# A decode step with its gradients: engine orders by hand, job loads on ScalarE, and w4 summed in the last forward heads

## The chip, the cores and the metric

The kernel runs on one core of a Trainium2 chip. The metric is the device time of one execution in microseconds (us), from the first to the last instruction with what lies around them. The time before the change is the median of three runs.

## The reference

One token (a vector of D = 640) goes through a block that a vector c conditions, and the function returns the block's output and the gradients of it against nine inputs. Cut to what matters:

```
mod = silu(c) @ w_mod                       # six vectors sa, ca, ga, sb, cb, gb of 640
h = layernorm(x) * (1 + ca) + sa
q = h @ wq                                  # 32 heads of 192
p = softmax(q . k_cache * 192**-0.5)        # 8192 keys a head
x1 = x + ga * ((p . v_cache) @ wo)
hb = layernorm(x1) * (1 + cb) + sb
out = x1 + gb * (hb + gelu(layernorm(hb) @ w3) @ w4)
```

The second block of the reference also has weights w1 and w2, but its shifted groups are all zero for a sequence of one token, so they add nothing. The gradients, for a given gradient of out, are those of x, k_cache, v_cache, wq, wo, w3, w4, c and w_mod. The two caches are 100 MB each in bf16; both are read (V twice, K once), and gradients of their size are written.

## The kernel before, in words

The keys of a head are laid over 128 partitions, 64 keys each, in two halves t = 0, 1 of 32 keys; a half of K or V is one DMA of 1.5 MB. The program has three stages.

**Forward (L395 to L444).** An iteration i works on three heads at once. Head i gets its scores: K times q on VectorE in four quarters (`prod`, L308 through L93), summed over 192 by ScalarE (`junk`, L313) for two quarters and by TensorE (`S_ps`, L316) for the other two. Head i-1 gets the maximum of its scores over all keys (L320 to L329, `mx_ps` and `negm`), its exp (`E_all`, L330), then `W` = V times E on VectorE (W0 and W1 for the halves, L93), and two products on TensorE that contract the keys of K with W: M1 (L349) for the first 128 of K's 192 columns and M2 (L363) for the rest. M1 and M2 hold what the gradient of q needs; by M2 also the attention's output comes out, through columns of K that GpSimd overwrites with ones (L354) after M1 has read them. Head i-2 gets its last M2 and its evictions and output (`fwd_out`). K halves use five buffers (`KV_sb`), V halves two. All these loads are issued by SyncE, in one queue: K (L159), V (L297), and in odd iterations W_o (L169), 480 KB of wo for this pair of heads, and W_c (L164), 480 KB of wq for the next pair's q. `q_bcast` makes q of two heads at a time (L264 on TensorE, L265 on ScalarE). In heads 1 to 6 a chunk of w_mod, also a `W_c`, is loaded and multiplied (`mod_chunk`, L248, with its copy L249).

**Middle (L450 to L568).** w4 and w3 are loaded, x1, two layernorms, w3, gelu, its derivative and the gradients back to `dao_c`, the gradient of the attention's projected output. The gradient that reaches gelu is a sum of w4 times a vector (`dg_part`, L470, twelve of them on VectorE).

**Backward (L749 to L787).** An iteration i loads V of head i again and multiplies it by `do_t` (L720 to L729, `dP_ps`), writes dV and dK as outer products by VectorE (`head_dv` L730, `head_dk` L734, issued from GpSimd, L714). The jobs of a pair of heads come beside it, every one and a half iterations: `pair_a` (L603) transposes W_o by TensorE (L612) and makes `do_t` and `qb_t`; `pair_b1` and `pair_b2` make the softmax's correction and the gradient of q; `pair_c` makes the gradients of wq and wo, `o_c` (L582) and `o_r` (L588), by ScalarE and writes them in ScalarE's DMA queue (L583, L589). Jobs for w_mod, w4 and w3 come in the last iterations.

What sets the order of the work: a scheduler of the framework takes the instructions in program order, and puts them in its own order on each engine's queue. Semaphores between engines and buffers decide when they start. The queues that matter here are SyncE's DMA queue (q1), ScalarE's (q10), GpSimd's (q0), and the instruction streams of the five engines.

Of the kernel before, what the change touches and what calls it, by code (L numbers as in the profile page):

```python
# [20 lines left out]
def kernel(  # L21
# [65 lines left out]

    V_ = nc.vector
# [73 lines left out]
    def load_cols(view, n):  # L162
        tl = ld.tile([P, NDC, CW], BF16, name="W_c", tag="ld")
        nc.sync.dma_start(out=tl, in_=view[:, :, n * CW : (n + 1) * CW])  # L164
        return tl

    def load_wo(g):
        tl = ld.tile([P, 3, D], BF16, name="W_o", tag="ld")
        nc.sync.dma_start(out=tl, in_=wo_v[g])  # L169
        return tl  # L170


    def colsum(vec, groups, out):
        ps = psum.tile([P, 512], FP32, tag="sm", name="cs_ps")
        n = groups * NDC
        PE_.matmul(ps[:, 0:n], lhsT=mean_f, rhs=vec, start=True, stop=True)
        V_.reduce_sum(out=out, in_=ps[:, 0:n].rearrange("p (g i) -> p g i", i=NDC), axis=AX.X)

    def layernorm(x_c, pfx, hook=None):
        mean = cvec(pfx + "_mean", 1)  # L180
        colsum(x_c, 1, mean)
        if hook:
            hook()
# [5 lines left out]
        colsum(sq, 1, var)  # L189
        if hook:  # L190
            hook()
        rstd = cvec(pfx + "_rstd", 1)
        std = cvec(pfx + "_std", 1)
        A_.activation(out=std, in_=var, func=ACT.Sqrt, bias=eps_c, scale=1.0)
        V_.reciprocal(out=rstd, in_=std)
# [4 lines left out]
    def layernorm_bwd(dn2, n, rstd, add_to, pfx):  # L200
        tt(dn2[:, 1, :], dn2[:, 0, :], n, ALU.mult)
        s = cvec(pfx + "_s", 2)
        colsum(dn2.rearrange("p g i -> p (g i)"), 2, s)
# [12 lines left out]
    def store_cols(dram_5p, col_f, name):  # L216
        ps = psum.tile([P, 512], FP32, tag="sm", name="st_ps")
# [25 lines left out]
    def mod_chunk(n):  # L243
        wt = load_cols(wm_v, n)
# [5 lines left out]

    n0, r0 = layernorm(x0_c, "ln0")
    NM0 = 4
    for n in range(NM0):
        mod_chunk(n)
# [12 lines left out]
    fq_cm = tc.tile_pool(name="fq", bufs=2)  # L267
# [3 lines left out]
    def q_pair(g):  # L271
        q_tiles[g] = fq.tile([P, CW], BF16, name="q_t")
        q_bcast(load_cols(wq_v, g), "q", q_tiles[g], bufs=1)

    q_pair(0)
# [9 lines left out]
    fp_cm = tc.tile_pool(name="fp", bufs=3)  # L285
    fp = fp_cm.__enter__()
    fv_cm = tc.tile_pool(name="fv", bufs=2)
    fv = fv_cm.__enter__()
    fw_cm = tc.tile_pool(name="fw", bufs=2)
    fw = fw_cm.__enter__()  # L290
    fsm_cm = tc.tile_pool(name="fsm", bufs=2)
    fsm = fsm_cm.__enter__()
# [7 lines left out]
    def fwd_mult(h, qi, st):  # L300
# [8 lines left out]
        if r == 0:  # L309
            for jj in range(JQ):  # L310
                j = qi * JQ + jj
                junk = fsm.tile([P, DH], BF16, name="junk")
                A_.activation(out=junk, in_=prod[:, jj, :], func=ACT.Copy, accum_out=st["S_h"][:, j : j + 1])  # L313
        else:
            for k in range(NDS):
                PE_.matmul(st["S_ps"][:, t, :, :], lhsT=ident_bf, rhs=prod[:, :, k * DS : (k + 1) * DS], start=(k == 0), stop=(k == NDS - 1))  # L316
# [26 lines left out]
    def fwd_m1(h, t, st):  # L343
        if t == 0:
# [3 lines left out]
        for j in range(JH):  # L348
            PE_.matmul(st["M1"][:, 0:DP], lhsT=kv[:, j, 0:P], rhs=W[:, j, 0:DP], start=(t == 0 and j == 0), stop=(t == 1 and j == JH - 1))  # L349
        if h % 2 == 0:  # L350
            ones = bass.AP(Kt.tensor, Kt.offset + DH, [list(Kt.ap[0]), [DH, JH], [1, 64]])
        else:
            ones = kv[:, :, 64:P]
        nc.gpsimd.memset(ones, 1.0)  # L354

    def fwd_m2(h, t, st):
        if t == 0:
# [4 lines left out]
        for j in range(JH):  # L362
            PE_.matmul(st["M2"][:, 0:DP], lhsT=Kt[:, j * DH + o : j * DH + o + P], rhs=W[:, j, 0:DP], start=(t == 0 and j == 0), stop=(t == 1 and j == JH - 1))  # L363

    def fwd_out(h, st):
        lo, olo = (0, 64) if h % 2 == 0 else (64, 0)
        g = h // 2
        A_.copy(out=M1_all[:, h, :], in_=st["M1"][:, 0:DP])
        oe = fsm.tile([1, DP], FP32, name="oe")
        A_.copy(out=oe, in_=st["M2"][olo : olo + 1, 0:DP])  # L370
        A_.copy(out=M2_all[lo : lo + 64, g, :], in_=st["M2"][lo : lo + 64, 0:DP])
        V_.reciprocal(out=rinv_all[0:1, h : h + 1], in_=oe[0:1, DH:DP])  # L372
        o_h = oe
        if h % 2 == 0:
            states["ops", g] = psum.tile([P, 512], FP32, tag="sm", name="o_ps")
        ops = states["ops", g]
# [372 lines left out]
    for i in range(-2, HQ):  # L749
# [27 lines left out]
        if i >= 0:  # L777
            head_dv(i)
# [40 lines left out]
```

## Time and profile before

| | |
|---|---|
| median of three runs | 1605.99 us (1593.37 to 1610.15) |
| profiled execution, its own time | 1602.02 us |
| its span | 1600.2 us |
| mean granted TensorE clock | 0.777 |
| busy: PE, DVE, ACT, POOL | 972.5, 1202.8, 619.6, 186.3 us |
| DMA moved | 574.62 MB, mean 359 GB/s |

How to read it: the stages lie one after another in the span, with the start until about 20 us, the forward loop until about 664, the middle until about 732 and the backward loop to the end. The busy times are sums over stages that have different limits, so each stage is read by itself. A DMA share is the mean busy share of the 16 DMA engines in a stretch. Names are those of the program (`KV_sb`, `V_sb`, `W_c`, ...), and L93 is a helper that records every tensor_tensor, so its rows are told apart by their tiles.

### The profile page before, as it was taken

To read this page: it belongs to the slowest core of one execution; us is meant where nothing else is said; L and a number is where in the kernel's file an instruction comes from. 1 tells how busy PE (TensorE), PEld (TensorE's weight loads), DVE (VectorE), ACT (ScalarE), POOL (GpSimd) and SP (SyncE) were. 2 spreads that over 40 slices of the span, in tenths; PEclk is the share of its full clock that TensorE was granted. 3 is DMA by queue.
4 is the path that set the end of the run, shared out by engine and by line. 5 is a ranking of instruction groups with operands and counts; after the bars stand their busy time and mean duration, and the time that the engine had idled before them with its cause. 6 is when DMAs were issued, how large, how long until landed. Compare 5 with 4: busy or idle time off the path is not lost.

```text
span 1600.2 us, 23161 instructions
## 1 busy us (share of the span) xinstructions
PE 972.5 (61%) x9043; PEld 823.7 (51%) x9043; DVE 1202.8 (75%) x1018; ACT 619.6 (39%) x2598; POOL 186.3 (12%) x203
## 2 busy tenths in 40 slices
PE   4878888888888888858444554464535563332541
PEld 3777777777777777856323342343324342222431
DVE  4677777666776666647994999399939998595977
ACT  5656666666666666423221312021302111312320
POOL 0111111111111111200100010000000001000010
PEclk9989999999999999978666676576657666566765
DMA  9789888888888888866998999899989999899998
GB/s 365 299 308 356 337 333 339 341 340 341 340 336 328 336 334 330 318 239 211 422 425 330 416 415 423 332 404 416 424 332 401 422 422 423 309 416 408 359 387 349
DMA packets 123115, 574.62 MB, mean 359 GB/s; under 512 B 7422, under 2 KB 81406, under 8 KB 82046
## 3 DMA queue, kind: packets, MB, share of 16 engines
q1 hardware_dynamic: 76798, 347.23, 55.9%
q0 software_dynamic: 18528, 201.34, 30.0%
q10 hardware_dynamic: 27680, 24.58, 4.4%
q8 instruction: 71, 1.16, 0.3%
q14 instruction: 38, 0.31, 0.0%
HBM read 347.21 MB, written 225.91 MB: 358 GB/s over the span
## 4 chain that ended last, share of the span: by engine, by line
DMA 45%; PE 22%; DVE 13%; ACT 9%; issue 7%; POOL 2%; SPq 1%; ACTq 0%; POOLq 0%; DVEq 0%
DMA W_o<-in_A_wo_dram 16%; DMA out_dram<-o_r 10%; DMA out_dram<-o_c 10%; DMA V_sb<-in_A_v_cache_dram 8%; PE M_ps L349 8%; ACT junk L313 6%; PE M_ps L363 4%; DVE W L93 3%; PE dP_ps L727 3%; DVE dK L93 2%; DVE KV_sb L93 2%; DVE prod L93 2%; POOL KV_sb L354 2%; ACT o_c L582 1%; PE S_ps L316 1%
## 5 line engine op out<-in xcount | busy, mean ns | idle before, releaser
L313 ACT ACTIVATE junk<-prod 128x192 bf16<-128x192 bf16 x1024 | 354.9, 349 | 121.1 <-DVE prod L93 121.1
L93 DVE TENSOR_TENSOR W<-V_sb,E_all 128x6144 bf16<-128x6144 bf16 x64 | 214.4, 3350 | 105.7 <-ACT E_all L330 102.4
L727 PE MATMUL dP_ps<-KV_sb,ident_bf 128*128 128x256 bf16 x1536 | 228.8, 320 | 99.5 <-DVE KV_sb L93 99.3
L349 PE MATMUL M_ps<-W,KV_sb 128*128 128x193 bf16 x2048 | 222.5, 271 | 69.8 <-DVE rinv_all L372 68.4
L727 PEld LDWEIGHTS <-ident_bf 128*128 128x128 bf16 x1536 | 174.9, 115 | 148.1 <-issue 74.2
L93 DVE TENSOR_TENSOR prod<-KV_sb,q_t 128x3072 bf16<-128x3072 bf16 x128 | 219.2, 1743 | 40.5 <-DMA KV_sb<-in_A_k_cache_dram 29.3
L349 PEld LDWEIGHTS <-KV_sb 128*128 128x128 bf16 x2048 | 200.0, 108 | 81.3 <-issue 75.2
L363 PE MATMUL M_ps<-W,KV_sb 128*128 128x193 bf16 x2048 | 194.7, 251 | 43.9 <-POOL KV_sb L354 43.2
L93 DVE TENSOR_TENSOR dV<-E_all,do_t 128x6144 bf16<-128x6144 bf16 x64 | 213.6, 3353 | 5.8 <-DMA out_dram<-dV 5.3
L93 DVE TENSOR_TENSOR KV_sb<-KV_sb,do_t 128x6144 bf16<-128x6144 bf16 x64 | 214.4, 3350 | 0.0
L93 DVE TENSOR_TENSOR dK<-dS,qb_t 128x6144 bf16<-128x6144 bf16 x64 | 212.1, 3352 | 2.7 <-DMA out_dram<-dK 2.6
L363 PEld LDWEIGHTS <-KV_sb 128*128 128x128 bf16 x2048 | 175.0, 99 | 57.0 <-POOL KV_sb L354 54.5
L313 ACT ACTIVATION_READ_ACCUMULATOR junk<-prod 128x1 f32 x1024 | 192.5, 188 | 0.0
L354 POOL MEMSET KV_sb<- 128x2048 bf16 x64 | 115.5, 1804 | 569.6 <-PE M_ps L349 556.1
L316 PE MATMUL S_ps<-prod,ident_bf 128*128 128x128 bf16 x1536 | 104.7, 225 | 11.1 <-DVE prod L93 11.1
L612 PE MATMUL wo_ps<-ident_bf,W_o 128*128 128x128 bf16 x240 | 21.3, 247 | 139.4 <-DMA W_o<-in_A_wo_dram 134.2
L666 ACT ACTIVATE vc<-dq_ps 128x384 bf16<-128x384 f32 x16 | 8.0, 498 | 250.8 <-PE dq_ps L664 250.8
L316 PEld LDWEIGHTS <-ident_bf 128*128 128x128 bf16 x1536 | 95.2, 101 | 12.5 <-issue 12.2
L612 PEld LDWEIGHTS <-W_o 128*128 128x128 bf16 x240 | 17.7, 111 | 144.5 <-DMA W_o<-in_A_wo_dram 139.2
L714 POOL DMA_DIRECT2D out_dram<-dK x64 | 34.0, 532 | 479.2 <-DVE dK L93 433.6
L736 DVE TENSOR_REDUCE dP<-dP_ps 128x64 f32<-128x512 f32 x32 | 21.9, 684 | 73.8 <-PE dP_ps L727 73.8
L582 ACT ACTIVATE o_c<-vc,ha_c 128x384 bf16<-128x384 bf16 x80 | 42.9, 604 | 70.1 <-DMA out_dram<-o_c 69.9
(198 smaller groups left out, 873.1 us busy)
## 6 DMA issues: line engine op xcount, KB each, us to landing
KV_sb<-in_A_k_cache_dram SPq DMA_DIRECT2D x64, 1536.0 KB, 8.3
V_sb<-in_A_v_cache_dram SPq DMA_DIRECT2D x64, 1536.0 KB, 11.2
KV_sb<-in_A_v_cache_dram SPq DMA_DIRECT2D x64, 1536.0 KB, 21.2
out_dram<-dV POOLq DMA_DIRECT2D x64, 1536.0 KB, 13.4
out_dram<-dK POOLq DMA_DIRECT2D x64, 1536.0 KB, 12.5
W_c<-in_A_wq_dram SPq DMA_DIRECT2D x32, 480.0 KB, 13.0
W_o<-in_A_wo_dram SPq DMA_DIRECT2D x32, 480.0 KB, 12.0
out_dram<-o_c ACTq DMA_DIRECT2D x30, 480.0 KB, 16.9
```

The costliest lines, as they stand in the source:

```text
L93: V_.tensor_tensor(out=out, in0=a, in1=b, op=op)
L313: A_.activation(out=junk, in_=prod[:, jj, :], func=ACT.Copy, accum_out=st["S_h"][:, j : j + 1])
L316: PE_.matmul(st["S_ps"][:, t, :, :], lhsT=ident_bf, rhs=prod[:, :, k * DS : (k + 1) * DS], start=(k == 0), stop=(k == NDS - 1))
L349: PE_.matmul(st["M1"][:, 0:DP], lhsT=kv[:, j, 0:P], rhs=W[:, j, 0:DP], start=(t == 0 and j == 0), stop=(t == 1 and j == JH - 1))
L354: nc.gpsimd.memset(ones, 1.0)
L363: PE_.matmul(st["M2"][:, 0:DP], lhsT=Kt[:, j * DH + o : j * DH + o + P], rhs=W[:, j, 0:DP], start=(t == 0 and j == 0), stop=(t == 1 and j ...
L582: A_.activation(out=o[:, i, :], in_=vec_bc, func=ACT.Copy, scale=col_f[:, i : i + 1])
L612: PE_.transpose(tps[:, k * P : (k + 1) * P], wo_t[:, cc, i * P : (i + 1) * P], ident_bf)
L666: A_.activation(out=v, in_=bps[:, 0:CW], func=ACT.Copy, scale=SCALE)
L714: nc.gpsimd.dma_start(out=dst_hd[h][:, t * JH : (t + 1) * JH, :], in_=o)
L727: PE_.matmul(dP_ps[:, t * JH : (t + 1) * JH, :], lhsT=ident_bf, rhs=V_sb[:, :, k * DS : (k + 1) * DS], start=(k == 0), stop=(k == NDS - 1))
L736: V_.reduce_sum(out=dP, in_=js.pop(("dP", h)), axis=AX.X)
```

## The change

The kernel is recorded in manual mode: the order of instructions on every engine is the order of the program's text, and the text is rewritten for it. The parts:

- The forward iteration is one function, `fwd_iter`, in which the three heads' steps are set by hand. The memset that puts ones over K is split in two, each after the half of M1 that read those columns; M2 is split in the same way. `q_pair` and `mod_chunk` come after the second quarter's sum and before exp. The pools of products and q lie on the other side of memory.
- w4 is loaded in iteration 32 (`tail_loads`), and nine of the twelve `dg_part` run between iterations 32 and 33. The other three stand in the layernorms.
- ScalarE's tables for the square root and tanh are loaded early by small activations.
- In the middle the w3 transposes are interleaved by hand, the first pair's `do_t` comes right after `dao_bf`, and x2 and `dao_bc` move into iteration 0 of the backward loop.
- In the backward loop the loads of W_o, W_c and w_mod are issued by ScalarE at the end of the iteration before (`job_loads(i + 1)`), no longer by SyncE at the top of an iteration. The jobs for w4 and w3 are spread over iterations 3, 6, ..., 24. The V product, dV and dK are interleaved by halves with the jobs.

The diff, cut to its core:

```diff
+    ctx.enter_context(tc.manual_schedule())
...
-    def load_cols(view, n):
+    def load_cols(view, n, eng=None):
         tl = ld.tile([P, NDC, CW], BF16, name="W_c", tag="ld")
-        nc.sync.dma_start(out=tl, in_=view[:, :, n * CW : (n + 1) * CW])
+        (eng or nc.sync).dma_start(out=tl, in_=view[:, :, n * CW : (n + 1) * CW])
         return tl
...
+    def fwd_iter(i, loads=None, tail=None):
...
+        for t in range(2):
+            if cur:
+                st["K"].append(K_first if (c, t) == (0, 0) else load_half(K_hd, c, t))
+            if prv:
+                load_v(p, t)
+        if loads:
+            loads()
+        wq_t = wm_n = None
+        if cur:
+            if c % 2 == 1:
+                states["wo", c // 2] = load_wo(c // 2)
+                if c + 1 < HQ:
+                    wq_t = load_cols(wq_v, (c + 1) // 2)
+            if 1 <= c <= NMC - NM0:
+                wm_n = load_cols(wm_v, NM0 + c - 1)
+            fwd_mult(c, 0, st)
+            fwd_accum(c, 0, 0, 7, st)
+        if prv:
+            fwd_max(p, pst)
+        if ppv:
+            fwd_m2(pp, 1, 0, ppst)
+            fwd_m2(pp, 1, 1, ppst)
+        if cur:
+            fwd_mult(c, 1, st)
+            fwd_sred(c, 1, st)
+        if wq_t is not None:
+            q_pair((c + 1) // 2, wq_t)
+        if wm_n is not None:
+            mod_chunk(NM0 + c - 1, wm_n)
+        if c == NMC - NM0 + 2:
+            dbo_prep()
+        if prv:
+            fwd_exp(p, pst)
+            fwd_ecol(p, 0, pst)
+        if ppv:
+            fwd_evict1(pp, ppst)
+        if cur:
+            fwd_accum(c, 0, 7, JQ, st)
+            fwd_mult(c, 2, st)
+        if ppv:
+            fwd_evict2(pp, ppst)
+        if prv:
+            fwd_ecol(p, 1, pst)
+            fwd_weighted(p, 0, pst)
+            fwd_m1(p, 0, 0, pst)
+            fwd_m1(p, 0, 1, pst)
...
+    fwd_iter(HQ, tail_loads)
+    sq_junk = cvec("sq_junk", 1)
+    A_.activation(out=sq_junk, in_=eps_c, func=ACT.Sqrt)
+    dg_part(9)
+    fwd_iter(HQ + 1)
...
-    at_a = {(3 * g) // 2 - 2: g for g in range(NG)}
-    i_ha = (3 * (NG - 1)) // 2 + 1
+    at_a = {(3 * g) // 2 - 1: g for g in range(1, NG)}
+    at_b = {(3 * g) // 2: g for g in range(NG)}
+    at_c = {(3 * g) // 2 + 1: g for g in range(NG)}
+    i_ha = max(at_c) + 1
...
+    def job_loads(i):
+        g = at_a.get(i)
+        if g is not None:
+            js["wo", g] = load_wo(g, A_)
+            js["wq", g] = load_cols(wq_v, g, A_)
         for n in mods.get(i, ()):
-            js["wm", n] = load_cols(wm_v, n)
+            js["wm", n] = load_cols(wm_v, n, A_)
...
+    for i in range(HQ):
+        ga, gb_, gc = at_a.get(i), at_b.get(i), at_c.get(i)
+        for t in range(2):
+            js["V", i, t] = load_half(V_hd, i, t)
+        v_product(i, 0)
+        if i == 0:
+            late_middle()
         if gb_ is not None:
             pair_b1(gb_)
+        v_product(i, 1)
+        dv(i, 0)
         if gb_ is not None:
             pair_b2(gb_)
+        if ga is not None:
+            wo_tr(ga, 0)
+            wo_tr(ga, 1)
+            pair_do(ga)
+        dv(i, 1)
+        ds(i)
+        dk(i, 0)
...
+        dk(i, 1)
+        if i in wjobs:
...
+        job_loads(i + 1)
```

Where instructions stand, at three places. First ScalarE in an odd forward iteration after head 8, from one run of accumulations to the last `W` column copy. Before:

```order
L313 ACTIVATE junk,S_h<-prod 128x192 x16
L265 ACTIVATE q_t<-q_ps 128x384
L368 COPY M_all<-M_ps 128x193
L313 ACTIVATE junk,S_h<-prod 128x192 x16
L330 ACTIVATE E_all<-S_h,negm 128x128
L370 COPY oe<-M_ps 1x193
L334 COPY W<-E_all 128x32
L371 COPY M_all<-M_ps 64x193
L334 COPY W<-E_all 128x32
```

After the change:

```order
L322 ACTIVATE junk,S_h<-prod 128x192 x23
L272 ACTIVATE q_t<-q_ps 128x384
L340 ACTIVATE E_all<-S_h,negm 128x128
L344 COPY W<-E_all 128x32
L377 COPY M_all<-M_ps 128x193
L322 ACTIVATE junk,S_h<-prod 128x192 x9
L382 COPY oe<-M_ps 1x193
L383 COPY M_all<-M_ps 64x193
L344 COPY W<-E_all 128x32
```

The eviction of q (`q_t`), which stood between two runs of sixteen accumulations, now stands directly ahead of exp (`E_all`).

Second, VectorE in an odd one of heads 1 to 6, from the sum of the scores to the second half of `W`. Before:

```order
L320 TENSOR_REDUCE S_h<-S_ps 128x2x16
L322 TENSOR_REDUCE m_996<-S_h 128x1
L93 TENSOR_TENSOR prod<-KV_sb,q_t 128x3072 x2
L329 TENSOR_REDUCE negm<-mx_ps 128x1
L93 TENSOR_TENSOR W<-V_sb,E_all 128x32x192
L372 RECIPROCAL rinv_all<-oe 1x1
L93 TENSOR_TENSOR prod<-KV_sb,q_t 128x3072
L385 COPY o_col<-o_ps 128x3
L93 TENSOR_TENSOR prod<-KV_sb,q_t 128x3072
L387 CAST o_cb<-o_col 128x3
L93 TENSOR_TENSOR W<-V_sb,E_all 128x32x192
L93 TENSOR_TENSOR ao_c<-ao_c,ao_ps 128x5
```

After the change:

```order
L330 TENSOR_REDUCE S_h<-S_ps 128x2x16
L332 TENSOR_REDUCE m_1631<-S_h 128x1
L94 TENSOR_TENSOR prod<-KV_sb,q_t 128x3072
L254 COPY mod_c<-mod_ps 128x3
L339 TENSOR_REDUCE negm<-mx_ps 128x1
L94 TENSOR_TENSOR prod<-KV_sb,q_t 128x3072
L94 TENSOR_TENSOR W<-V_sb,E_all 128x32x192
L483 RECIPROCAL rinv_all<-oe 1x1
L94 TENSOR_TENSOR prod<-KV_sb,q_t 128x3072
L402 COPY o_col<-o_ps 128x3
L404 CAST o_cb<-o_ps 128x3
L94 TENSOR_TENSOR W<-V_sb,E_all 128x32x192
```

The copy of the modulation's chunk (`mod_c`), which stood behind the last of these rows, now stands ahead of `negm`, the input of exp; the third product stands ahead of the first `W`.

Third, ScalarE in the backward loop, from one pair's gradients of wq and wo to the next pair's `woT`, after the change:

```order
L711 ACTIVATE o_c<-vc,ha_c 128x384 x5
L712 DMA out_dram<-o_c 128x5x384
L717 ACTIVATE o_r<-dao_bc,o_col 128x640 x3
L718 DMA out_dram<-o_r 128x3x640
L170 DMA W_o<-in_A_wo_dram 128x3x640
L165 DMA W_c<-in_A_wq_dram 128x5x384
L587 COPY woT<-wo_ps 128x1024
```

And SyncE there before:

```order
L159 DMA KV_sb<-in_A_v_cache_dram 128x6144 x2
L164 DMA W_c<-in_A_wq_dram 128x5x384
L169 DMA W_o<-in_A_wo_dram 128x3x640
L159 DMA KV_sb<-in_A_v_cache_dram 128x6144 x4
L164 DMA W_c<-in_A_wq_dram 128x5x384
```

The loads of W_o and W_c stood among the V loads on SyncE; they now stand behind the writes of `o_c` and `o_r` on ScalarE, and SyncE has V loads alone.

More of the change, by code (lines that the diff above doesn't have):

```diff
@@ L445 @@
-    for cm in (fsm_cm, fw_cm, fv_cm, fp_cm, fq_cm):
+            fwd_mult(c, 3, st)
+            fwd_sred(c, 3, st)
+        if ppv:
+            fwd_o(pp, ppst)
+            if pp % 2 == 1:
+                fwd_ocol(pp // 2)
+        if prv:
+            fwd_weighted(p, 1, pst)
+        if tail:
+            tail()
+        if ppv and pp % 2 == 1:
+            fwd_ao(pp // 2)
+        if prv:
+            fwd_m1(p, 1, 0, pst)
+            fwd_m1(p, 1, 1, pst)
+        if ppv:
+            states.pop(pp)
@@ L475, in fill @@
[L475 to L486 removed]
+        big["tr", n] = tps
```

466 lines of the change are left out of this document (237 added, 229 removed).

## The prediction

> **What bounds the kernel now.** I read the windows by stage first, then the chain that ended last, then the engines' timelines where the chain points. The windows have, per stage, the busy time of PE, PEld, DVE, ACT and POOL, then the granted TensorE clock, the DMA share and GB/s.
>
> ```profile
> 462.00:503.00 41.00, 33.65 (x387) 31.55 (x385) 29.09 (x24) 26.34 (x141) 7.22 (x4) 0.92 0.86 333
> 664.00:732.00 68.00, 44.80 (x536) 40.31 (x535) 27.07 (x92) 17.44 (x32) 6.07 (x4) 0.75 0.62 234
> 732.00:1600.00 868.00, 398.31 (x2433) 288.35 (x2431) 719.15 (x532) 179.22 (x316) 69.14 (x130) 0.66 0.96 389
> ```
>
> The forward (first row, one pair of heads) has nothing near full: DMA 0.86, PE 34 of 41 us. It is a loop of waits. The middle (second row) is a string of short dependent steps. The backward (third row) is bound by DMA, 0.96, which leaves about 35 us without it in 868. The chain of waits shows the forward's period, and SyncE's list of waits what closes the loop:
>
> ```profile
> 462.02 11.24 DMA V_sb<-in_A_v_cache_dram
> 502.99 11.56 DMA V_sb<-in_A_v_cache_dram
> ```
>
> ```profile
> SPq L159 <- PE M_ps L363: 478.6, 59, 11.3
> ```
>
> One pair takes 502.99 - 462.02 = 40.97 us, and the K loads (L159) wait 59 times for the end of M2 (L363), the last reader of their buffer. So the loop is: M2 ends, K is loaded, product, exp, W = V*E, M1, M2. SyncE's timeline shows the loads of an odd head behind that release, with the issue time in the first column:
>
> ```profile
> 484.90 0.33 SPq L159 DMA_DIRECT2D KV_sb<-in_A_k_cache_dram  x1
> 485.34 0.37 SPq L297 DMA_DIRECT2D V_sb<-in_A_v_cache_dram  x1
> 485.76 0.42 SPq L169 DMA_DIRECT2D W_o<-in_A_wo_dram  x1
> 486.24 0.80 SPq L164 DMA_DIRECT2D W_c<-in_A_wq_dram  x1
> ```
>
> W_c, the columns of wq for the next pair's q, is last of four. The DMA view of this window (KB, us from issue to landing), and W_c's and K's own views (lowest, median, highest; K's is the second) give the landings:
>
> ```profile
> W_c<-in_A_wq_dram SPq DMA_DIRECT2D x1, 480.0 KB, 12.6
> ```
>
> ```profile
> DMA to landing us min/median/max: 10.6/12.9/13.2
> ```
>
> ```profile
> DMA to landing us min/median/max: 6.6/8.3/10.0
> ```
>
> From the K issue to W_c in place are 486.24 + 12.6 - 484.90 = 13.95 us. What uses it now, on PE, ACT and DVE:
>
> ```profile
> 499.65 0.97 PE L264 MATMUL q_ps<-W_c,ha_bf 128*128 128x384 bf16 x5
> 500.46 2.03 PE L363 MATMUL M_ps<-W,KV_sb 128*128 128x193 bf16 x22
> ```
>
> ```profile
> 489.40 0.39 ACT L330 ACTIVATE E_all<-S_h,negm 128x128 bf16<-128x128 f32 x1
> 500.66 0.49 ACT L265 ACTIVATE q_t<-q_ps 128x384 bf16<-128x384 f32 x1
> ```
>
> The q matmuls slip into M2 once W_c is there, and this head's exp was over 10 us before: today nothing of this head waits for W_c.
>
> **The change part by part: forward.** The hand order puts q_pair between S and M1 on PE, and q_t ahead of exp on ACT. So in an odd iteration exp, W0 (the first half of W) and M1 stand behind a load that is the last of four. Prices are the rows above and these:
>
> ```profile
> 489.82 3.36 DVE L93 TENSOR_TENSOR W<-V_sb,E_all 128x6144 bf16<-128x6144 bf16 x1 [1.68 <-ACT E_all L330]
> 493.17 1.73 DVE L93 TENSOR_TENSOR prod<-KV_sb,q_t 128x3072 bf16<-128x3072 bf16 x1
> ```
>
> ```profile
> 489.53 2.90 PE L363 MATMUL M_ps<-W,KV_sb 128*128 128x193 bf16 x32 [0.38 <-POOL KV_sb L354]
> 494.01 2.81 PE L349 MATMUL M_ps<-W,KV_sb 128*128 128x193 bf16 x31
> ```
>
> ```profile
> 473.97 0.32 PE L349 MATMUL M_ps<-W,KV_sb 128*128 128x193 bf16 x1 [3.51 <-DVE rinv_all L372]
> 475.04 4.93 PE L349 MATMUL M_ps<-W,KV_sb 128*128 128x193 bf16 x31
> ```
>
> M1 costs 2.81 us, and 4.93 us where PE stood idle for 3.51 us ahead of its first matmul. Count from the end of the second W (W1) of the iteration before. M2 ended about then (W0's end + M1 2.81 + M2 2.90 + 0.04), so K goes out at 0.3 and W_c is in place at 14.25. q 0.97 and its hand-over: 15.3; q_t: 15.9; exp: 16.35; W0: 19.75. PE is idle from 15.3 to 19.75, so M1 takes 4.9 and M2 2.9: the next K goes out 8.0 after W0, at 27.75. The even head has no W_c: K 6.6, product 1.73, W0 3.36, so W0 ends at 39.45; then the third product and W1, 5.3 with hand-overs: 44.8, and with the second K issue's 0.3, 45.15. A pair costs 45.15 against 40.97. From both sides: W_c at its lowest 10.6 and M1 at full clock give about 41, K at its median 8.3 gives 46.9. I take +4.2, the row of this very place (12.6); 12 pairs: **+50** (0 to +72).
>
> In heads 1 to 6 each iteration also has a chunk of the modulation. Its load is behind W_c, its matmuls stand ahead of M1 on PE, its copy ahead of negm on DVE. Before, they stand between and after other work:
>
> ```profile
> 111.41 0.52 PE L248 MATMUL mod_ps<-sc_bf,W_c 128*128 128x1 bf16 x15
> ```
>
> ```profile
> 112.73 0.14 DVE L249 COPY mod_c<-mod_ps 128x3 f32<-128x3 f32 x1
> ```
>
> One more 480 KB at 333 GB/s is 1.5 us. Odd head: chunk in place about 16, matmuls and copy 16.75, negm and exp 17.5, W0 20.9, next K 28.9. Even head, now waiting too (one 480 KB load fewer ahead of it: chunk in place 13.95 - 1.5 = 12.4 after the K issue): W0 17.2 after that issue, next K 25.2 after it. The pair is 28.6 + 25.2, near 54. Three pairs at +13.6: **+41**; if DVE's copy is covered, +13.
>
> Without the W_c wait the order itself would be quick: with W0 17.3 us from K issue to the next K issue, a pair near 36. The memset split in two lets M2's first half go while M1 ends (POOL's 1.8 us between them leaves the path); that gain is in the sum above, and is lost in the wait.
>
> **Middle.** The stretch runs from the last full W to the first V product:
>
> ```profile
> 660.47 3.34 DVE L93 TENSOR_TENSOR W<-V_sb,E_all 128x6144 bf16<-128x6144 bf16 x1
> 731.70 3.35 DVE L93 TENSOR_TENSOR KV_sb<-KV_sb,do_t 128x6144 bf16<-128x6144 bf16 x1
> ```
>
> ```profile
> L470 DVE CUSTOM_DVE_ANT_0 jk<-w_sb,dbo_bc 128x640 bf16<-128x640 bf16 x12 | 9.9, 824 | 0.4
> ```
>
> ```profile
> 713.58 1.28 ACT L512 ACT_TABLE_LOAD   x1
> ```
>
> ```profile
> 724.39 2.50 PE L214 MATMUL dao_ps<-ident_f,dao_c 128*128 128x128 f32 x10
> ```
>
> That is 67.9 us. The twelve w4 sums (9.9 us) run on DVE there; nine move into the last forward head, three into gaps of the layernorms: -8, since two PE transposes and u still take a little. Tanh's table is loaded early: -1.3. dao_bc's matmuls and the W_o transposes behind them leave the path to do_t: -2.5 and about -4. The last M2 and evictions: -4 to -8 from the tighter drain. Together **-20** (-15 to -24). What hides the nine sums is DVE's wait for the last head's loads.
>
> **Backward.** The engines do the same work; the W_o and W_c loads move from SyncE's queue (q1, among the V loads) to ScalarE's (q10), behind the o_c and o_r writes. The DMA view of 780 to 790 us has packets, MB and share by queue, and W_o's landing time is in its own view:
>
> ```profile
> q0 software_dynamic: 337, 3.74, 87.6%
> q10 hardware_dynamic: 335, 0.26, 7.5%
> q1 hardware_dynamic: 334, 0.26, 7.5%
> ```
>
> ```profile
> DMA to landing us min/median/max: 8.9/27.2/44.7
> ```
>
> ```profile
> 1020.61 1.04 PE L612 MATMUL wo_ps<-ident_bf,W_o 128*128 128x128 bf16 x8 [35.36 <-DMA W_o<-in_A_wo_dram]
> 1028.96 0.69 DVE L736 TENSOR_REDUCE dP<-dP_ps 128x64 f32<-128x512 f32 x1 [23.96 <-PE dP_ps L727]
> ```
>
> ```profile
> 1020.00:1030.00 10.00, 9.39 (x69) 7.47 (x69) 1.04 (x4) 0.00 (x0) 0.00 (x0) 0.72 0.29 98
> ```
>
> Three queues were served one packet each in turn, whatever the packet's size: 11 KB on q0, 0.78 KB on q10. The rows of W_c and o_c (128x5) make 640 small packets, those of W_o and o_r (128x3) 384: 2048 a pair, all on q10 now, 1024 before. At 335 in 10 us that is 61 us, where a pair of jobs comes each 1.5 heads, 1.5 x 868/32 = 41 us. PE meets W_o in order, and dP stands behind it, as the two stall rows show (PE 35 us, then DVE 24 us); at the end of the stall, once W_o has landed, DMA is at 0.29 for 10 us, a tail of 7 us without it. The 35 us idle of the whole stage are five such tails. A backlog on q10 drains fast once q0 is empty, since a small packet takes 0.075 x 160 / 335 = 0.04 us of an engine, so only the idle tail is lost. Bounds: all 35 us idle gone, -35; one tail in each of 15 pairs in place of five, +70. I take ten tails, **+35**, since W_o's landing, already up to 44.7 us, is the row nearest to it.
>
> The Trainium skill, page "DMA: Bandwidth & Descriptors", section "Queues, rings and completion order", says that each DMA engine goes round the queues that have work, packet by packet; the three equal counts agree. Its section "Issuing engines are not separate DMA queues" says that issuing from several engines saves only the issue time; by that the move would be worth nothing and the sum 35 us lower, 1673, and no row here has SyncE's issue time as the limit.
>
> **Sum:** 1602.02 (this execution; 4 below the median of the runs) + 50 + 41 - 20 + 35 = 1708.
>
> **The rivals.**
> First, faster: the W_c wait decides nothing, because the load lands before exp's other inputs are ready (for: W_c has landed in 10.6; against: it is issued last of four). Then a forward pair is bound by its K buffers at 36: 15 x -5 = -75, middle -20, backward 0: 1507; with half of that gain, and a backward between 0 and +35, 1545 to 1580. It decides once W_c is in place about 8 us after the K issue. 17%.
> Second, no change: W_c at its lowest, pairs near 41, chunks +13, middle -20, backward +10: about 1605. 9%.
> Third, ScalarE's queue collapses: o_c's buffers are also awaited on ACT, so woT and do_t stand behind writes as well; backward +70 to +110: 1743 to 1783. For it: 2048 packets in 41 us; against: do_t is asked for later and later, as pairs of jobs come every 1.5 heads and are used every 2. 17%.
> The forecast itself, 1625 to 1742, has 57%.
>
> **How the numbers follow.** Range: from the middle of the first rival, 1565, to the middle of the third, 1765; about a tenth lies outside on each side. A measurement of this kernel tells about 1% from no change: faster 0.17 (the first), same 0.09 (the second), slower 0.74 (the forecast and the third).
>
> **What would show it.** Right: a forward pair near 45, in odd heads PE idle until W_c lands and ACT waiting ahead of q_t, then exp; pairs of heads 1 to 6 near 54; the middle near 48; DMA share of the backward below 0.96, W_o on ACT's queue landing later than 27 us at the median, and wo_ps waiting for it. Wrong: W_c landed before the S matmuls end (forward near 36), or a backward of 868 us or less.

## The result

| | before | after the change |
|---|---|---|
| median | 1602.42 us (1593.37 to 1610.15, 4 runs) | 1861.24 us (1852.99 to 1868.78, 4 runs) |
| profiled execution, its span | 1602.02, 1600.2 us | 1864.54, 1862.8 us |
| forward, to the end of head 30's W | 663.8 us | 829.5 us |
| middle, to the first V product | 67.9 us | 45.3 us |
| backward, to the end | 868.5 us | 988.1 us |

The ratio is 1.1616, with a 95% interval from 1.1531 to 1.1702: slower by 16%. The stages begin and end as in the prediction. The forward gives +165.7 us, the middle -22.6, the backward +119.5, together the 262.6 us between the spans. Of the two runs of the kernel `q late` below, the one that took 1.7% longer is counted as slow and left out.

The forward before, and then the three stages of the changed kernel (PE, PEld, DVE, ACT, POOL busy, then clock, DMA share, GB/s):

```profile
20.00:664.00 644.00, 523.70 (x6006) 491.00 (x6006) 450.97 (x366) 419.41 (x2248) 110.05 (x61) 0.93 0.87 334
```

```profile
20.00:829.00 809.00, 565.10 (x6022) 525.84 (x6021) 451.93 (x363) 417.91 (x2249) 115.98 (x122) 0.81 0.72 266
829.00:875.00 46.00, 38.35 (x435) 33.97 (x436) 26.39 (x86) 16.44 (x29) 5.71 (x6) 0.72 0.82 313
875.00:1862.00 987.00, 387.70 (x2516) 276.54 (x2514) 730.12 (x542) 183.70 (x318) 69.78 (x131) 0.65 0.86 343
```

DMA's share fell from 0.87 to 0.72 in the forward and from 0.96 to 0.86 in the backward, while the engines do the same work. So both long stages wait more. VectorE and ScalarE are as long at their work as before; TensorE took 565.10 us for the forward's matmuls in place of 523.70, at a granted clock of 0.81 in place of 0.93.

**The forward.** SyncE's timeline has one W_o load per pair of heads. The first and the last of a stretch of eleven pairs after the modulation's chunks:

```profile
253.02 0.42 SPq L170 DMA_DIRECT2D W_o<-in_A_wo_dram  x1
...
803.23 0.43 SPq L170 DMA_DIRECT2D W_o<-in_A_wo_dram  x1
```

(803.23 - 253.02) / 11 = 50.0 us a pair, 41.0 before. One odd head, on SyncE, PE, ACT and DVE:

```profile
601.36 0.33 SPq L160 DMA_DIRECT2D KV_sb<-in_A_k_cache_dram  x1
602.70 0.73 SPq L165 DMA_DIRECT2D W_c<-in_A_wq_dram  x1
```

```profile
615.71 1.76 PE L271 MATMUL q_ps<-W_c,ha_bf 128*128 128x384 bf16 x5 [5.42 <-DMA W_c<-in_A_wq_dram]
621.82 5.33 PE L360 MATMUL M_ps<-W,KV_sb 128*128 128x193 bf16 x32 [4.35 <-DVE W L94]
631.36 0.38 PE L398 MATMUL o_ps<-rinv_all,oe 1*128 1x1 f32 x2
```

```profile
617.50 0.49 ACT L272 ACTIVATE q_t<-q_ps 128x384 bf16<-128x384 f32 x1 [12.70 <-PE q_ps L271]
617.89 0.39 ACT L340 ACTIVATE E_all<-S_h,negm 128x128 bf16<-128x128 f32 x1
```

```profile
618.31 3.36 DVE L94 TENSOR_TENSOR W<-V_sb,E_all 128x6144 bf16<-128x6144 bf16 x1 [8.25 <-ACT E_all L340]
631.78 0.16 DVE L402 COPY o_col<-o_ps 128x3 f32<-128x3 f32 x1 [7.79 <-PE o_ps L398]
631.92 3.35 DVE L94 TENSOR_TENSOR W<-V_sb,E_all 128x6144 bf16<-128x6144 bf16 x1
```

Two waits stand here. The first is the one foretold: q starts 14.35 us after the K issue, once W_c is there, q_t and exp follow, and DVE has stood for 8.25 us. The second was not in the sum: o_col, a 0.16 us copy, stands ahead of the second half of W on DVE and waits 7.79 us for o_ps, which on PE stands behind M1, M2 and a score sum.

**The backward.** Three rows of the changed kernel's list of waits (us in total, times, longest):

```profile
PE wo_ps L586 <- DMA W_o<-in_A_wo_dram: 238.1, 14, 26.1
DVE pc L94 <- PE dc_ps L604: 184.8, 14, 17.4
DVE o_col L402 <- PE o_ps L398: 115.3, 16, 8.7
```

(The third is the forward's.) In 14 of 15 pairs PE waits for W_o, 17 us in the mean, and DVE at `pc` for `dc_ps`, which needs W_o and, by its place on PE behind q, also W_c. One such wait on ACT's queue, PE and DVE:

```profile
1063.62 0.49 ACT L272 ACTIVATE qb_t<-q_ps 128x384 bf16<-128x384 f32 x1 [16.05 <-PE q_ps L271]
1069.83 0.50 ACTq L170 DMA_DIRECT2D W_o<-in_A_wo_dram  x1
```

```profile
1097.87 1.78 PE L586 MATMUL wo_ps<-ident_bf,W_o 128*128 128x128 bf16 x15 [24.25 <-DMA W_o<-in_A_wo_dram]
```

```profile
1083.76 3.35 DVE L94 TENSOR_TENSOR KV_sb<-KV_sb,do_t 128x6144 bf16<-128x6144 bf16 x1
1102.83 0.16 DVE L94 TENSOR_TENSOR pc<-dc_ps,o_col 128x3 f32<-128x3 f32 x1 [15.72 <-PE dc_ps L604]
```

ACT has waited for the last pair's W_c (through q and qb_t) until 1063.62, and only then reaches o_c, o_r and, at 1069.83, this pair's W_o. It lands 28 us later. DVE is at pc, the first step that needs it, 17 us after the issue (1083.76 + 3.35 = 1087.1), and stands until 5 us after the landing. Every second pair is like this one: in the other seven DVE comes to pc 30 us after the issue.

### The profile page after: what moved, and what is told of

The parts are those of the page before. It is cut to its first block, busy times and chain, and to the rows that moved or that the text cites. A ratio compares the mean times of both kernels' runs of the same rounds, so it can differ in the third digit from the quotient of the medians.

```text
span 1862.8 us, 23297 instructions
## 1 busy us (share of the span) xinstructions
PE 996.8 (54%) x9043; PEld 840.4 (45%) x9043; DVE 1214.3 (65%) x1017; ACT 621.6 (33%) x2601; POOL 192.6 (10%) x267
## 4 chain that ended last, share of the span: by engine, by line
issue 48%; PE 20%; DVE 13%; DMA 13%; POOL 4%; SPq 1%; ACT 1%; POOLq 0%; DVEq 0%; ACTq 0%
PE M_ps L360 10%; DMA W_c<-in_A_wq_dram 10%; DVE W L94 9%; PE M_ps L374 5%; POOL out_dram L816 3%; DMA W_c<-in_w_mod_dram 3%; DVE prod L94 2%; PE q_ps L271 1%; PE S_ps L326 1%; DMA W_o<-in_A_wo_dram 1%; DVE KV_sb L94 1%; DVE dV L94 1%; PE dP_ps L829 0%; SPq L170 0%; SPq L304 0%
## 5 line engine op out<-in xcount | busy, mean ns | idle before, releaser
L360 PE MATMUL M_ps<-W,KV_sb 128*128 128x193 bf16 x2048 | 257.6, 303 | 152.2 <-DVE W L94 72.7
L360 PEld LDWEIGHTS <-KV_sb 128*128 128x128 bf16 x2048 | 231.0, 121 | 174.0 <-issue 145.3
L829 PE MATMUL dP_ps<-KV_sb,ident_bf 128*128 128x256 bf16 x1536 | 218.7, 312 | 89.6 <-DVE KV_sb L94 89.6
L364 POOL MEMSET KV_sb<- 128x960 bf16 (+1 forms) x128 | 121.7, 951 | 726.3 <-PE M_ps L360 726.2
L374 PE MATMUL M_ps<-W,KV_sb 128*128 128x193 bf16 x2048 | 187.4, 248 | 0.0
L374 PEld LDWEIGHTS <-KV_sb 128*128 128x128 bf16 x2048 | 177.2, 99 | 2.9
L586 PE MATMUL wo_ps<-ident_bf,W_o 128*128 128x128 bf16 x240 | 26.3, 294 | 238.1 <-DMA W_o<-in_A_wo_dram 238.1
L587 ACT COPY woT<-wo_ps 128x1024 bf16<-128x1024 bf16 (+1 forms) x32 | 29.2, 962 | 355.7 <-PE wo_ps L586 355.7
L586 PEld LDWEIGHTS <-W_o 128*128 128x128 bf16 x240 | 22.7, 137 | 241.4 <-DMA W_o<-in_A_wo_dram 241.4
L271 PE MATMUL q_ps<-W_c,ha_bf 128*128 128x384 bf16 x160 | 51.0, 476 | 143.3 <-DMA W_c<-in_A_wq_dram 143.3
L723 PE MATMUL acc_ps<-W_c,ident_bf 128*128 128x480 bf16 x104 | 45.2, 588 | 149.5 <-DVE W_c L94 149.5
L326 PE MATMUL S_ps<-prod,ident_bf 128*128 128x128 bf16 x1536 | 99.7, 223 | 7.0 <-DVE prod L94 7.0
## 6 DMA issues: line engine op xcount, KB each, us to landing
W_c<-in_A_wq_dram SPq DMA_DIRECT2D x17, 480.0 KB, 12.8
```

Of the source, the lines that this page charges most:

```text
L271: PE_.matmul(qps[:, 0:CW], lhsT=ha_bf[:, i : i + 1].to_broadcast([P, P]), rhs=wt[:, i, :], start=(i == 0), stop=(i == NDC - 1))
L326: PE_.matmul(st["S_ps"][:, qi // 2, :, :], lhsT=ident_bf, rhs=st["prod", qi][:, :, k * DS : (k + 1) * DS], start=(k == 0), stop=(k == NDS ...
L586: PE_.transpose(tps[:, k * P : (k + 1) * P], js["wo", g][:, cc, i * P : (i + 1) * P], ident_bf)
L587: A_.copy(out=js["woT", g].rearrange("p i n -> p (i n)")[:, b0 * P : b1 * P], in_=tps[:, 0 : (b1 - b0) * P])
L723: PE_.matmul(acc[:, 0 : NDC * 96].rearrange("p (i d) -> p i d", d=96), lhsT=ident_bf, rhs=wt[:, :, k * 96 : (k + 1) * 96], start=(first an ...
L829: PE_.matmul(dP_ps[:, t * JH : (t + 1) * JH, :], lhsT=ident_bf, rhs=V_sb[:, :, k * DS : (k + 1) * DS], start=(k == 0), stop=(k == NDS - 1))
```

## The experiments

All times of stages in this section are from profiled executions, cut as above. "Forward" is to the end of head 30's W, "pair" is the spacing of W_o loads over the same eleven pairs.

| kernel | span | forward | middle | backward | pair |
|---|---|---|---|---|---|
| before | 1600.2 | 663.8 | 67.9 | 868.5 | 41.0 |
| after the change | 1862.8 | 829.5 | 45.3 | 988.1 | 50.0 |
| o_col behind W | 1822.1 | 780.3 | 46.6 | 995.3 | 47.1 |
| q late | 1740.3 | 721.5 | 44.2 | 974.5 | 41.5 |
| q late, o_col behind W | 1695.3 | 667.5 | 46.6 | 981.2 | 38.4 |
| chunks late | 1826.5 | 807.6 | 45.1 | 973.9 | |
| w4 sums in the middle | 1879.4 | 826.2 | 49.8 | 1003.4 | |
| dc_ps early | 1891.2 | 825.1 | 44.8 | 1021.3 | |
| job loads on SyncE | 1750.0 | 829.6 | 45.0 | 875.4 | |
| job loads an iteration earlier | 1756.0 | 824.5 | 45.0 | 886.5 | |
| writes on GpSimd | 1766.6 | 829.6 | 45.0 | 892.0 | |
| four moves together | 1545.2 | 623.2 | 45.2 | 876.8 | 38.2 |
| and o_ps early | 1556.5 | 641.7 | 48.1 | 866.8 | 39.6 |

A caution for reading it: each row is one execution, and where the backward's code and loads are the change's own, its time still ranges from 974 to 1003 us. Differences below 30 us are not read in that stage.

**o_col behind W.**

```diff
-            if pp % 2 == 1:
-                fwd_ocol(pp // 2)
         if prv:
             fwd_weighted(p, 1, pst)
+        if ppv and pp % 2 == 1:
+            fwd_ocol(pp // 2)
```

> The changed kernel with one move: the copy of o_ps to o_col (and o_cb) stands behind the second half of W on VectorE, no longer ahead of it. Theory A (the second half of W in odd heads waits for o_ps, which on TensorE stands behind M1, M2 and a score sum): that half ends some 8 us sooner, a forward pair falls from 50 to about 45 us, about 1861 - 16 x 5 = 1785 us. Theory B (only the W_c load ahead of exp and the K release after M2 set the period): the pair stays at 50, 1861 us.

1827.05 us median, ratio to before 1.1397 (1.1289 to 1.1506). The pair fell by 2.9 us, in the direction of theory A, to 47.1 and not 45, and the time is about halfway between the theories. DVE's timeline shows why less came back:

```profile
593.34 3.36 DVE L94 TENSOR_TENSOR W<-V_sb,E_all 128x6144 bf16<-128x6144 bf16 x1 [8.19 <-ACT E_all L340]
598.93 3.35 DVE L94 TENSOR_TENSOR W<-V_sb,E_all 128x6144 bf16<-128x6144 bf16 x1
606.24 0.16 DVE L402 COPY o_col<-o_ps 128x3 f32<-128x3 f32 x1 [3.95 <-PE o_ps L398]
607.15 1.75 DVE L94 TENSOR_TENSOR prod<-KV_sb,q_t 128x3072 bf16<-128x3072 bf16 x1
```

The second W now follows without a wait, but o_col waits behind it, and the next head's first product behind o_col.

**q late, alone.**

```diff
-        if wq_t is not None:
-            q_pair((c + 1) // 2, wq_t)
         if wm_n is not None:
             mod_chunk(NM0 + c - 1, wm_n)
...
             fwd_m2(p, 0, 1, pst)
+        if wq_t is not None:
+            q_pair((c + 1) // 2, wq_t)
         if cur:
             fwd_mult(c, 3, st)
```

> The changed kernel with one move: q of the next pair stands behind the first half's M2 on TensorE, and its eviction behind the third run of accumulations on ScalarE, no longer ahead of exp; o_col stays where the change put it. Theory A (both waits count, and they overlap in time): exp no longer waits for W_c, the first half of W ends 12 us after the K issue in place of 20, the pair falls to 40 to 42 us, about 1861 - 15 x 9 = 1726 us. Theory B (o_col alone decides): 1861 us, or at most 30 less.

1742.05 us. The pair fell to 41.5: theory A. The wait for W_c ahead of exp is worth 8.5 us a pair.

**Both** (the two edits above in one kernel).

> Both moves together. Theory A: a pair is bound by the K buffers (load 6.6, product, W, M1, M2: 18 us a head, 36 to 38 a pair), about 1861 - 15 x 12.5 = 1673 us. Rival (M1 at half clock and VectorE's own sequence hold it at what it was before the change, 41 us a pair): about 1726 us.

1707.71 us median, ratio 1.0653 (1.0359 to 1.0946). The pair is 38.4, nearer to theory A's bound by the K buffers than to its rival's 41; the time is above theory A's 1673, near the rival's 1726. The two gains add: 2.9 + 8.5 = 11.4 us, measured together 11.6. In the odd heads of this kernel W starts right behind the product that waited for K, and q's matmuls find W_c in place:

```profile
544.74 3.35 DVE L94 TENSOR_TENSOR W<-V_sb,E_all 128x6144 bf16<-128x6144 bf16 x1
```

```profile
548.24 4.20 PE L360 MATMUL M_ps<-W,KV_sb 128*128 128x193 bf16 x32 [2.75 <-DVE W L94]
...
555.30 0.97 PE L271 MATMUL q_ps<-W_c,ha_bf 128*128 128x384 bf16 x5
...
568.39 2.88 PE L360 MATMUL M_ps<-W,KV_sb 128*128 128x193 bf16 x32 [2.34 <-DVE rinv_all L481]
```

**Chunks late.**

```diff
-        if wm_n is not None:
-            mod_chunk(NM0 + c - 1, wm_n)
         if c == NMC - NM0 + 2:
...
         if prv:
             fwd_weighted(p, 1, pst)
+        if wm_n is not None:
+            mod_chunk(NM0 + c - 1, wm_n)
```

> The changed kernel with one move: the modulation's chunk (matmuls and copy) behind the second half of W in heads 1 to 6. Theory A (chunk ahead of M1 and of negm costs 13 us a pair, as predicted): the first three pairs fall by 30 to 41 us together, 1820 to 1832 us. Theory B (W_c, one load ahead of the chunk, has held the odd heads already, and only the even heads gain): 12 to 20 us, about 1845 us.

1838.29 us median, ratio 1.1461 (1.1385 to 1.1537). The profiled execution, 36 us shorter, looks like theory A, but 14 of these 36 us are in the backward, within its spread. The forward fell by 21.9, next to theory B. With the W_c wait of the odd heads gone (and o_col moved), the same move is worth 667.5 - 623.2 = 44.3 us (the kernels with two and with four moves), so the waits cover each other in part.

**Job loads on SyncE.**

```diff
-            js["wo", g] = load_wo(g, A_)
-            js["wq", g] = load_cols(wq_v, g, A_)
+            js["wo", g] = load_wo(g)
+            js["wq", g] = load_cols(wq_v, g)
...
-            js["wm", n] = load_cols(wm_v, n, A_)
+            js["wm", n] = load_cols(wm_v, n)
```

> The changed kernel with the loads of W_o, W_c and w_mod in the backward loop issued by SyncE at the same place of the program, one iteration ahead; the forward as in the change. Theory A (ScalarE's queue, with 2048 small packets a pair, makes the loads late): W_o and W_c land sooner, the stalls on W_o and on dc_ps vanish, the backward falls from 988 us to 870 to 890, in all 1742 to 1763 us. Theory B (the place in the program and the hand order of TensorE decide, dc_ps behind q behind W_c, whichever queue carries the load): less than a third of the 120 us comes back, 1820 to 1861 us.

1750.00 us median, ratio 1.0917 (1.0836 to 1.0997). The backward fell by 112.7 us to 875.4, theory A, with the change's order of everything else. Landing, and the stage's window:

```profile
W_o<-in_A_wo_dram SPq DMA_DIRECT2D x13, 480.0 KB, 15.0
```

```profile
875.00:1750.00 875.00, 390.82 (x2515) 278.87 (x2513) 729.96 (x542) 183.66 (x318) 69.78 (x131) 0.69 0.95 387
```

W_o lands after 15.0 us where it took 27, and DMA is at 0.95 again. But three things change with the queue: what is ahead of the load in it, how many small packets it must carry, and which engine has to come to the issue. The next kernel tries what the late load holds up, and the two after it change the time of the issue and what is ahead of the load.

**dc_ps early.**

```diff
+        cps = psum.tile([P, 512], FP32, tag="sm", name="dc_ps")
+        for k in range(3):
+            PE_.matmul(cps[:, k : k + 1], lhsT=do_t[0:1, k * P : (k + 1) * P], rhs=ones_bf[0:1, 0:1], start=True, stop=True)
+        js["cps", g] = cps
         q_t = bst.tile([P, CW], BF16, name="qb_t", bufs=7)
         q_bcast(js["wq", g], "bc", q_t, bufs=2)
         js["q", g] = q_t
-        cps = psum.tile([P, 512], FP32, tag="sm", name="dc_ps")
...
```

> The changed kernel with one move in the backward: the three dc_ps matmuls ahead of q's on TensorE, so that they wait for W_o and not for W_c. Theory A (VectorE stands at pc for dc_ps, which stands behind q's matmuls and W_c): of its 185 us of waits a third or more goes, 1780 to 1820 us. Theory B (TensorE still stands at q for W_c, and the V products' sums behind it; the stall moves to the next instruction on VectorE): under 20 us, about 1850 us.

1890.99 us median, ratio 1.1790 (1.1761 to 1.1818). Theory A falls. No time came back; 33 us more stand in the backward, beyond that stage's spread, and where they come from stays open. Its waits:

```profile
PE wo_ps L586 <- DMA W_o<-in_A_wo_dram: 320.0, 14, 27.4
DVE pc L94 <- PE dc_ps L601: 204.3, 13, 17.5
```

Freed from W_c, dc_ps and pc wait as long, and PE waits 82 us more for W_o: in this kernel it is the W_o load that is late. In the change itself both loads are: at four of the fourteen waits PE had stood only 1 to 6 us for W_o, and DVE then waited for W_c, behind q.

**Job loads an iteration earlier, still on ScalarE.**

```diff
-    ld = ctx.enter_context(tc.tile_pool(name="ld", bufs=4))
+    ld = ctx.enter_context(tc.tile_pool(name="ld", bufs=5))
...
             js["V", i, t] = load_half(V_hd, i, t)
+        job_loads(i + 1)
         v_product(i, 0)
...
-        job_loads(i + 1)
```

> The changed kernel with the backward's job loads still on ScalarE's queue, but issued at the top of the iteration before, a whole iteration (27 us) earlier, with five buffers for them in place of four. Theory A (lead time: a load that lands 27 us after its issue is asked for 17 us after it, and ScalarE can issue it only once it has passed the last pair's wait for W_c): the stalls vanish, backward 870 to 900 in place of 988, 1742 to 1775 us. Theory B (the queue's share: 2048 small packets a pair of jobs do not go through one queue in 41 us while the other two are busy, however early they are issued): the stalls stay, 1825 us or more.

1756.26 us median, ratio 1.0972 (1.0823 to 1.1121). The backward is 886.5: theory A, lead time, by the total. DMA's view of its backward from 875 us on, and its row of pc:

```profile
q10 hardware_dynamic: 49067, 43.29, 14.3%
...
W_o<-in_A_wo_dram ACTq DMA_DIRECT2D x14, 480.0 KB, 36.4
```

```profile
DVE pc L94 <- PE dc_ps L604: 100.0, 7, 15.3
```

The queue carries its 49,067 small packets, a W_o load takes even longer, 36.4 us at the median, and 102 us come back all the same. So theory B falls by its own number, 1825 us or more. But the stalls did not vanish, as theory A had it: seven of fourteen are left, in the pairs whose load is asked for 42 to 54 us after its issue and lands after up to 58.6. For every second pair the lead is still too short, so this run does not show that the queue has room to spare. The edit also adds a fifth buffer, which was not tried by itself.

**Writes on GpSimd.**

```diff
-        A_.dma_start(out=dram, in_=o)
+        nc.gpsimd.dma_start(out=dram, in_=o)
```

(in both `cols_job` and `rows_job`.)

> The changed kernel with the writes of o_c and o_r issued by GpSimd, so that ScalarE's queue holds only the loads; their place in ScalarE's order is the change's. Theory A' (the loads are late because they are behind the writes in one queue): W_o lands 12 to 15 us after its issue in place of 27, and the backward falls by 90 us or more, to 1775 us or less. Theory B' (they are issued late, behind qb_t, o_c and o_r on ScalarE): landing is short but the stalls stay in part, 1800 to 1840 us. A loss that neither speaks of: GpSimd stands for o_c ahead of a dK write.

1771.66 us median, ratio 1.1068 (1.0912 to 1.1224). With the loads alone in ScalarE's queue, issued where the change issues them:

```profile
W_o<-in_A_wo_dram ACTq DMA_DIRECT2D x15, 480.0 KB, 11.2
```

```profile
DVE pc L94 <- PE dc_ps L604: 48.4, 7, 7.8
```

W_o lands after 11.2 us at the median (some 4 us in every second pair, 18 to 20 in the others), the backward falls by 96 us to 892, theory A'; seven short waits are left. Not only the landing changed: with the writes gone DVE comes to pc 28 and 36 us after the issue, no longer 17 and 30. So this run does not part what the queue costs from what the blocked engine costs.

Together the three kernels show what the loss is: two times, the landing of W_o and W_c behind their issue, and the time until DVE asks for what they make. In the pair shown above that is 28.0 us to land, 5.0 from there to pc, less a lead of 17.3: 15.7 us of wait. Either side can be mended: a shorter landing, or a longer lead.

**w4 sums back in the middle.**

```diff
-dg_part(9)
     fwd_iter(HQ + 1)
...
+    dg_part(9)
     u = cvec("u", NFC)
```

> The changed kernel with the nine early w4 sums put back behind n2_bf in the middle, as they stood before the change; w4 is still loaded in the last forward heads. Theory A (the sums were on the path of the middle and are covered by the last forward head's waits now): 7 to 8 us more, 1868 us by span. Theory B (they only fill VectorE's time, TensorE's transposes and the layernorms set the middle): 0 to 2 us more.

1876.34 us median, ratio 1.1698 (1.1656 to 1.1741). The middle grew by 4.5 us, to 49.8, between the theories, where it lies between 44.2 and 48.1 in the other kernels. So the nine sums were at most partly on its path. The rest of the 17 us is in the backward's spread.

**Four moves together** (q late, o_col behind W, chunks late, job loads on SyncE):

> The changed kernel with four moves: q late and o_col behind W (as before in this series), the modulation's chunk and its copy behind the second half of W in heads 1 to 6, and the backward's loads of W_o, W_c and w_mod on SyncE. If the losses are the three found and add up: 1695 (span with q late and o_col moved) - 113 (the loads, measured alone) - 30 to 40 (chunks) = 1542 to 1552 us, 3 to 4% faster than before the change. Rival (the losses overlap, above all the backward's, which also starts earlier): 1580 to 1610 us, no faster than before.

1548.10 us median (1546.94 to 1550.42), ratio 0.9657 (0.9638 to 0.9675): 3.4% faster than before the change, where the sum of the losses put it. The windows by stage:

```profile
20.00:623.00 603.00, 504.34 (x5970) 483.28 (x5970) 450.79 (x362) 415.92 (x2249) 116.11 (x122) 0.94 0.92 356
623.00:668.00 45.00, 36.52 (x488) 32.95 (x486) 26.15 (x87) 15.70 (x28) 5.71 (x6) 0.84 0.88 321
668.00:1545.00 877.00, 395.78 (x2518) 282.36 (x2516) 731.02 (x542) 184.32 (x320) 70.02 (x131) 0.68 0.95 387
```

Against before, the forward gains 40.6 us, the middle 22.7, and the backward gives 8.3 back.

**And o_ps early.**

```diff
             V_.reciprocal(out=rinv_all[0:1, pp : pp + 1], in_=ppst["oe"][0:1, DH:DP])
+            fwd_o(pp, ppst)
...
-        if ppv:
-            fwd_o(pp, ppst)
```

> The kernel with all four moves (1548 us) and one more: o_ps's two matmuls stand behind the first half's M1 on TensorE, ahead of M2, q and the score sum, so that o_col, behind the second half of W, finds them done (it waited 4 us in each odd head). Theory A (that wait delays the next head's first product and so the pair): a pair falls from 37.7 to about 36.5 us, 1525 to 1535 us. Theory B (the K buffers' loop, load, product, W, M1, M2, sets the pair and the wait is covered): 1545 to 1550 us.

1558.81 us median, ratio 0.9730 (0.9689 to 0.9772): slower than without the move, so theory A falls, and theory B's 1545 to 1550 does not hold either. o_col hardly waits any more, but the next step on DVE does, for ao_ps, 62.6 us in 16 times:

```profile
DVE ao_c L94 <- PE ao_ps L413: 62.6, 16, 5.1
```

ao_ps stands on PE behind q and the score sum just as o_ps had. The wait moved on by one step, and the forward took 18.5 us longer, which the matmuls put between M1 and M2 may be part of; that was not tried by itself.

## Why the prediction was wrong

The sign was right, and the W_c wait, the chunks and the backward's loads were named as the places of loss, but the size was far off: +106 forecast, +262.6 measured between the spans.

**The pairs after the chunks: +50 forecast, +116.6 measured.** Eleven of these twelve pairs gave (50.0 - 41.0) x 11 = +99, the first of them +17.6; `dbo_prep` stands ahead of exp there, in head 8, and what it costs was not tried. The W_c wait had its mechanism and its size right: the prediction put the pair without it at 36 and with it at 45.15, a wait of 9; taking q away gave 8.5 to 8.7. From the odd head's K issue to the even head's the sum has 27.45 us, and the timeline 629.96 - 601.36 = 28.6. What is left of the pair is the even head:

```profile
629.96 0.33 SPq L160 DMA_DIRECT2D KV_sb<-in_A_k_cache_dram  x1
...
652.13 0.33 SPq L160 DMA_DIRECT2D KV_sb<-in_A_k_cache_dram  x1
```

```profile
641.28 1.75 DVE L94 TENSOR_TENSOR prod<-KV_sb,q_t 128x3072 bf16<-128x3072 bf16 x1
642.94 3.35 DVE L94 TENSOR_TENSOR W<-V_sb,E_all 128x6144 bf16<-128x6144 bf16 x1
```

The step that failed is "The even head has no W_c: K 6.6, product 1.73, W0 3.36, so W0 ends at 39.45", 11.7 us behind its K issue; measured it ends 16.3 behind it (646.3 - 629.96), and the next K goes out after 22.2 us, not 17.7. The sum had this head wait for K. K was there at about 636.6 (6.6 us after its issue), and the product took it up at 641.28 with no wait: VectorE came late, since o_col had held it until 631.78 in the odd head, with the second W and the even head's first products behind. The sum had passed over that o_col, though the order rows quoted ahead of it show the copy there. Moved, it gives back 2.9 us a pair and not its 7.79 us of waiting, for K bounds the gain to 641.28 - 636.6 = 4.7. The other 2 us of the miss are the base: 38.4 in place of 36, with M1 at 4.20 us after 2.75 us of idle PE where the bound had full speed in both heads.

**Heads 1 to 6: +41 forecast, +39.9 measured.** The W_o loads of heads 1 and 7, before and after the change, bound these three pairs:

```profile
14.73 5.58 SPq L169 DMA_DIRECT2D W_o<-in_A_wo_dram  x1
...
158.52 0.38 SPq L169 DMA_DIRECT2D W_o<-in_A_wo_dram  x1
```

```profile
11.93 0.38 SPq L170 DMA_DIRECT2D W_o<-in_A_wo_dram  x1
...
195.59 0.38 SPq L170 DMA_DIRECT2D W_o<-in_A_wo_dram  x1
```

143.8 us became 183.7. The term held, and it let the two waits overlap: in its odd head the chunk puts the next K only 1.15 us behind the W_c path, and the even head pays for the rest. Moving the chunks gave 22 us back, as the run above shows, and not the whole term. (By the prediction's own 28.6 + 25.2 the gain of a pair is 12.8 and not 13.6, which changes little.) The pairs themselves are not near 54: they took 69.3, 59.7 and 54.6 us, where 58.3, 44.6 and 40.9 stood before, so the agreement is partly luck. The 9 us that are left of the forward's growth lie at its two ends.

**Middle: -20 forecast, -22.6 measured.** The sum held. Of its parts only nine of the twelve w4 sums were tried by themselves: 4.5 us, where the term for all twelve was 8.

**Backward: +35 forecast, +119.5 measured.** The step that failed is the tail count: "The 35 us idle of the whole stage are five such tails" and "I take ten tails". Counted in windows of 1 us, DMA falls idle at only three waits before the change, for 19 us in all. After it, it does so at eleven of the fourteen waits, for 6.4 to 9.5 us each and 89 in all. So the term is eight tails more of 8 us, +70, and not five more of 7. By the stage's shares DMA is idle for 0.14 x 987 = 138 us in place of 35, 103 more; where the 33 us beyond the waits lie, and the 16 us beyond the idle time, stays open. The rival with +70 to +110 (a chance of 17%) came nearest, but by its size and not by its reason: ScalarE, which was to wait for o_c's buffers, lost 0.5 us to them in the pairs' part of the stage.

Behind the wrong count is a wrong deadline. The prediction worked out that 2048 packets in 41 us were more than the queue's turn, and expected W_o to land later than 27 us. Landings did not change:

```profile
DMA to landing us min/median/max: 16.9/27.1/35.4
```

They were 27.2 at the median before. What changed is the lead. Before, DVE came to a pair's pc 105 to 129 us after its W_o was issued (pairs 3 to 15, save the 75 us of the first), so a late load held PE but never pc. In the change it comes after 17 or 30 us: the load goes out only after qb_t, which waits for the last pair's W_c, and after o_c and o_r, and pc follows one iteration on. The prediction looked at do_t, "asked for later and later"; pc is the first to ask. The order rows of ScalarE showed what stands ahead of the issue; the prediction counted packets in its queue and not what blocks the engine that issues them.

How a stall becomes lost time is as foretold, a tail with no DMA. The DMA views of 1055 to 1060, of 1062 to 1067 and of 1067 to 1070 us:

```profile
q0 software_dynamic: 186, 2.09, 97.9%
q10 hardware_dynamic: 87, 0.06, 3.6%
```

```profile
q0 software_dynamic: 2, 0.01, 0.6%
```

```profile
q10 hardware_dynamic: 656, 0.49, 48.2%
```

While the gradient writes of q0 last, W_c's packets get 87 turns in 5 us. Both are done at about 1062, q's matmuls start at 1061.8, and for 5 us DMA moves two packets. It starts again with o_c, which ScalarE writes at 1066.66, behind qb_t; the next gradient write is issued at 1070.78.

The Trainium skill, page "DMA: Bandwidth & Descriptors", section "Issuing engines are not separate DMA queues", says that issuing from several engines saves only the time on the sequencer. The runs differ from it: the same loads at the same place of the program, issued by SyncE and not by ScalarE, are worth 113 us here. On ScalarE they stand behind the writes in its queue and behind the engine's own waits, and the two kernels with an earlier issue and with the writes moved gave 102 and 96 us back.

## What to carry to other kernels

In a hand-written order every small instruction that takes its input from another engine is a gate for all that stands behind it on its engine: cost it by when its input is ready on the other engine, and not by its own 0.16 us. For a load that is moved to another engine's queue, compare two times, from the issue to the landing there and from the issue to the first use, and look for the issue behind what that engine itself waits for. Waits in one loop overlap, so measure each move alone and together: o_col and q added up, the chunks were worth 22 us beside the W_c wait and 44 without it.

## What the runs showed of the hardware that was not expected

A queue of small packets was slow beside a busy queue of large ones and quick without it. The DMA view of 1035 to 1040 us of the changed kernel has ScalarE's queue with 994 packets and 1.09 MB in 5 us, where q0 had all but run out of work (15 packets):

```profile
q10 hardware_dynamic: 994, 1.09, 60.3%
```

That is eleven times the 87 packets of the 5 us quoted above, so the landing time of such a load says more of the other queues than of its own size. TensorE ran slower behind many of the forward's gaps: M1 took 2.88 us after 2.34 us of idle, 4.20 after 2.75 and 5.33 after 4.35. The length of the gap alone does not set it: in the kernel with both moves M1 also took 4.50 us after 2.34 us of idle, and 2.88 after 2.75. The forward's mean granted clock went from 0.93 before to 0.81 with the change and 0.94 with the four moves, and its matmuls took 523.70 us before, 565.10 and 504.34. A wait in the forward thus can cost twice, once as it stands and again in the matmuls behind it.
